# Window attention and MoE: one moving block for both parts of the probabilities, a full-width stationary block for global scores, interleaved first steps

## The chip, the cores and the metric

The kernel runs on one core of one Trainium2 chip. The metric is the device time in microseconds (us) of one execution; the time before is 1079.34 us, the median of three runs (1076.82 to 1079.34). Engines: PE is the matmul engine, DVE the vector engine, ACT the scalar engine, POOL the general one, and SP here only issues DMAs. Matmul results land in PSUM, which has 8 banks of 512 float32 columns on 128 partitions.

## The reference

Attention over 8 batches and 8 heads of 64 dimensions: 512 local tokens that see a window of 32 to each side and 32 global tokens, and 32 global tokens that see all 544. Its output goes through a feed-forward pair of layers (MoE in the names; there is one expert).

```python
k_all = np.concatenate([k_g, k_l], axis=2)
v_all = np.concatenate([v_g, v_l], axis=2)
s_g = scale * np.matmul(q_g, k_all.transpose(0, 1, 3, 2))
out_g = np.matmul(sm(s_g), v_all)
s_ll = scale * np.matmul(q_l, k_l.transpose(0, 1, 3, 2))
s_ll = np.where(np.abs(pos[:, None] - pos[None, :]) <= window, s_ll, -1e9)
s_lg = scale * np.matmul(q_l, k_g.transpose(0, 1, 3, 2))
out_l = np.matmul(sm(np.concatenate([s_lg, s_ll], axis=-1)), np.concatenate([v_g, v_l], axis=2))
x = np.concatenate([out_g, out_l], axis=2)   # then (batch * 544, 512)
h = x @ w_in                                 # 512 -> 2048
return ((h / (1.0 + np.exp(-h))) @ w_out)    # 2048 -> 512
```

## The kernel before

**Two strands on one PE queue.** The MoE runs over 34 tiles of 128 tokens, in a first block of one tile and eleven blocks of three (`SIZES`, L38). In a block, `first_layer` makes 128 of the 2048 hidden units at a time (16 rounds f) and `second_layer` of the round before adds them into the output banks. Attention makes the tiles of the next block meanwhile: 128 steps k, one for each batch b, chunk c of 128 queries and pair pr of heads.

**Split numbers.** Most operands are float32 that is split in a high part, rounded to the PE's fast float32 form, and the low rest; a product is then hi x hi + hi x lo + lo x hi. The first steps use plain float32 instead: scores until k = 28 (`ND`), values until k = 16 (`KF`), global scores until batch 3 (`GF`), and the first MoE block.

**A step.** `st_load` and `st_vload` fetch, `st_split` and `st_vsplit` split. `st_scores` makes the scores of two heads in bank s; DVE reduces and masks them (L351), ACT exponentiates, DVE and ACT normalize, and a DMA brings the probabilities into `rr`. `st_turn` transposes them into bank t; ACT writes the high part `pt_hi` (L403) and DVE the low part `pt_lo` (L404), POOL adds the 32 columns of global queries. `st_out` multiplies with the values: `vv` holds a chunk's values as 128 stationary columns, 64 high and 64 low. For each of two heads u and two key blocks a, a matmul of `vv` with `pt_hi` (L438) gives hi x hi on partitions 0 to 63 and lo x hi on 64 to 127, and a second one of the high values alone with `pt_lo` (L440) adds hi x lo. Both heads lie side by side in bank o. ACT copies the lower half out (L460), and DVE adds the upper one (L461) into `xs`, from which `xh` and `xl` are split (L462, L463).

**Heads of the global queries.** `g_load`, `g_split`, `g_scores` prepare a batch's global queries a batch ahead: three matmuls for each half of 272 keys (L245 to L247) in banks s and o, copied by ACT into `pgs` (L248). `g_soft` normalizes, `g_turn` transposes (gt in bank o, gu in bank s).

**Order.** PE's order is the program's. Each part of a step has a due time in steps (`DUE`, `HEAD`, `TURN`, `LATE`, L49 to L55), the stream is sorted by it, and `fill` issues what is due: by three parts after each first layer and by one after each output tile. So time in steps is spread over a block's matmuls. The other engines' orders are laid by a scheduler. In the first steps (k below 4) everything waits `LAG` more, and batch 0's global scores come after them. After the first block, banks s, t and o have one buffer each (`attbank`, L76); a step that needs a bank waits until DVE and ACT have emptied it.

**Weights.** 32 half loads of 512 KB, issued on ACT's queue (`fetch_weights`, L170), arrive as 64-bit words that `join_weights` makes into float32 on ACT (L196) and DVE (L198, L199).

Of the kernel before, what the change touches and what calls it, by code (L numbers as in the profile page):

```python
# [59 lines left out]
def attention_moe_kernel(ctx: ExitStack, tc: tile.TileContext, qk0_in, qk_in, v_in, gqk, wts, out):  # L60
# [63 lines left out]
    pts = []  # L124

    def pt_tiles(k):
        if not pts:
            for part in ("hi", "lo"):
                pts.append(work.tile([P, 2, 2, P + SG], F32R, tag=f"pt_{part}", name=f"pt_{part}"))
                nc.gpsimd.memset(pts[-1].bitcast(F32), 0.0)  # L130
        return pts

    def pt_whole(k):
        return work.tile([P, 2, 2, P + SG], F32, tag="pt_lo" if k % 2 else "pt_hi", name=f"pt{k}")
# [35 lines left out]
    def fetch_weights():  # L170
# [49 lines left out]
    def g_split(b, p):  # L220
        if b < GF:
# [3 lines left out]
        nc.scalar.copy(out=hi[:, :GW], in_=raw[:, :GW])  # L225
        nc.vector.tensor_tensor(out=lo, in0=raw[:, QG:GW], in1=hi[:, QG:GW].bitcast(F32), op=ALU.subtract)
        nc.vector.tensor_tensor(out=hi[:, GW : GW + QG], in0=raw[:, :QG], in1=hi[:, :QG].bitcast(F32),
                                op=ALU.subtract)
        state["gqk", p] = hi, lo

    def g_scores(b, p):
# [4 lines left out]
        else:  # L236
            hi, lo = state.pop(("gqk", p))
            qh, ql, kh = hi[:, :QG], hi[:, GW : GW + QG], hi[:, QG:GW]
        for j, kind in enumerate("so"):
            s = attbank(kind, f"gs{j}_{b}_{p}")  # L240
            ks = slice(j * GH, (j + 1) * GH)
            if b < GF:
                nc.tensor.matmul(s[:QG, :GH], raw[:, :QG], raw[:, QG:GW][:, ks], start=True, stop=True)  # L243
            else:
                nc.tensor.matmul(s[:QG, :GH], qh, kh[:, ks], start=True, stop=False)  # L245
                nc.tensor.matmul(s[:QG, :GH], qh, lo[:, ks], start=False, stop=False)
                nc.tensor.matmul(s[:QG, :GH], ql, kh[:, ks], start=False, stop=True)  # L247
# [479 lines left out]
```

## Time and profile before

| what | value |
|---|---|
| median of three runs | 1079.34 us |
| the profiled execution, its own time | 1074.63 us |
| its span in the profile | 1072.8 us |
| first MoE matmul | at 28.47 us |
| first matmul of the second block | at 110.39 us |
| mean granted PE clock | 0.989 |

A row of the timeline has the start in us, the busy time in us, engine, line, operation, out<-in, shape and count, and in brackets the idle time of the engine before it with what ended it. A matmul's shape is rows x stationary columns, then partitions x moving columns. A row of groups has the count, the total busy time in us and the mean in ns. Matmuls overlap in the pipeline, so the distance from one start to the next is what a matmul takes of PE's time. DVE's and ACT's rows overlap by less than 0.1 us.

### The profile page before, as it was taken

To read this page: it belongs to the slowest core of one execution; us is meant where nothing else is said; L and a number is where in the kernel's file an instruction comes from. 1 tells how busy PE (TensorE), PEld (TensorE's weight loads), DVE (VectorE), ACT (ScalarE), POOL (GpSimd) and SP (SyncE) were. 2 spreads that over 40 slices of the span, in tenths; PEclk is the share of its full clock that TensorE was granted. 3 is DMA by queue.
4 is the path that set the end of the run, shared out by engine and by line. 5 is a ranking of instruction groups with operands and counts; after the bars stand their busy time and mean duration, and the time that the engine had idled before them with its cause. 6 is when DMAs were issued, how large, how long until landed. Compare 5 with 4: busy or idle time off the path is not lost.

```text
span 1072.8 us, 19856 instructions
## 1 busy us (share of the span) xinstructions
PE 1037.6 (97%) x6168; PEld 929.6 (87%) x6168; DVE 748.4 (70%) x2285; ACT 735.1 (69%) x1977; POOL 189.0 (18%) x480
## 2 busy tenths in 40 slices
PE   6899989999999999999999999999999999999997
PEld 4676879889999899989999888999999999999996
DVE  3788756777788677786658877787877787664322
ACT  4788877777687677776558777777777777654322
POOL 2002766211111111111001111111111111110000
PEclk7999999999999999999999999999999999999999
DMA  7796232443343344333224334343433433310000
GB/s 258 242 320 207 90 94 79 130 138 100 109 147 118 100 135 129 111 114 104 76 76 150 127 98 130 113 124 123 128 111 115 152 105 113 115 40 21 30 1 29
DMA packets 67305, 126.01 MB, mean 117 GB/s; under 512 B 7552, under 2 KB 27520, under 8 KB 67200
## 3 DMA queue, kind: packets, MB, share of 16 engines
q1 hardware_dynamic: 62592, 107.97, 31.8%
q10 hardware_dynamic: 4608, 16.78, 4.5%
q8 instruction: 49, 0.80, 0.3%
q14 instruction: 56, 0.46, 0.1%
HBM read 86.44 MB, written 8.91 MB: 89 GB/s over the span
## 4 chain that ended last, share of the span: by engine, by line
PE 85%; ACT 5%; DVE 5%; DMA 2%; issue 2%; POOL 1%; SPq 0%; ACTq 0%; DVEq 0%
PE h L600 33%; PE out L625 11%; PE out L627 10%; PE out L626 10%; PE s L347 5%; PE o L438 4%; PE o L440 3%; PE t L382 3%; DMA raw<-in_qk_dram 1%; PE o L434 1%; PE h L594 1%; ACT probs L355 1%; PE gs L243 1%; ACT w_hi L209 1%; PE gt L281 1%
## 5 line engine op out<-in xcount | busy, mean ns | idle before, releaser
L600 PE MATMUL h<-xh,w_hi 128*128 128x384 f32 x704 | 241.5, 343 | 0.0
L600 PE MATMUL h<-xl,w_hi 128*128 128x384 f32 x704 | 238.5, 339 | 0.2 <-DVE xl L451 0.2
L600 PE MATMUL h<-xh,w_lo 128*128 128x384 f32 x704 | 238.3, 339 | 0.0
L625 PE MATMUL out<-w_hi,gh 128*128 128x512 f32 x528 | 219.0, 415 | 0.0
L627 PE MATMUL out<-w_hi,gl 128*128 128x512 f32 x528 | 208.5, 395 | 0.3 <-DVE gl L613 0.3
L626 PE MATMUL out<-w_lo,gh 128*128 128x512 f32 x528 | 207.8, 393 | 0.0
L606 ACT ACTIVATE t<-h 128x384 f32<-128x384 f32 (+1 forms) x192 | 90.8, 473 | 155.0 <-PE h L600 147.6
L608 DVE SCALAR_TENSOR_TENSOR t<-t,h 128x384 f32<-128x384 f32 x176 | 97.2, 552 | 108.0 <-ACT t L606 106.7
L600 PEld LDWEIGHTS h<-xl,w_hi 128*128 128x128 f32 x704 | 133.0, 189 | 5.9 <-DVE xl L451 0.5
L600 PEld LDWEIGHTS h<-xh,w_hi 128*128 128x128 f32 x704 | 132.9, 189 | 5.3
L600 PEld LDWEIGHTS h<-xh,w_lo 128*128 128x128 f32 x704 | 132.6, 188 | 0.0
L613 DVE TENSOR_TENSOR gl<-t,gh 128x384 fp32r<-128x384 f32 x176 | 100.4, 570 | 42.5 <-PE out L627 36.0
L355 ACT ACTIVATE probs<-probs,st 128x224 f32<-128x224 f32 x244 | 115.8, 476 | 9.3 <-DVE st L351 7.9
L406 POOL CAST pt_hi<-pgt 128x64 fp32r<-128x64 f32 x112 | 37.5, 335 | 478.2 <-PE o L440 334.5
L627 PEld LDWEIGHTS out<-w_hi,gl 128*128 128x128 f32 x528 | 99.2, 188 | 23.7 <-DVE gl L613 0.7
L351 DVE CUSTOM_DVE_ANT_0 probs<-s,mask 128x224 f32<-128x224 f32 x244 | 85.1, 384 | 44.2 <-PE s L347 39.2
L625 PEld LDWEIGHTS out<-w_hi,gh 128*128 128x128 f32 x528 | 99.7, 189 | 12.0 <-issue 1.6
L626 PEld LDWEIGHTS out<-w_lo,gh 128*128 128x128 f32 x528 | 100.0, 189 | 10.5
L612 ACT CAST gh<-t 128x384 fp32r<-128x384 f32 x176 | 89.8, 510 | 23.9 <-DVE t L608 21.2
L317 ACT CAST qk<-raw 128x704 fp32r<-128x704 f32 x100 | 78.0, 780 | 17.8 <-PE s L347 15.2
L461 DVE TENSOR_TENSOR xs<-o,xs 64x160 f32<-64x160 f32 x224 | 70.6, 315 | 26.9 <-ACT xs L460 22.6
L438 PE MATMUL o<-pt_hi,vv 128*128 128x160 f32 x448 | 87.8, 264 | 0.5 <-DVE xs L461 0.2
(120 smaller groups left out, 1878.3 us busy)
## 6 DMA issues: line engine op xcount, KB each, us to landing
raw<-in_qk_dram SPq DMA_DIRECT2D x100, 352.0 KB, 3.0
rr<-probs SPq DMA_DIRECT2D x112, 256.0 KB, 2.3
vraw<-in_v_dram SPq DMA_DIRECT2D x128, 128.0 KB, 2.3
raw_w<-in_wts_dram ACTq DMA_DIRECT2D x32, 512.0 KB, 6.3
raw_g<-in_gqk_dram SPq DMA_DIRECT2D x32, 304.0 KB, 2.9
out_dram<-o SPq DMA_DIRECT2D x32, 256.0 KB, 2.6
raw<-in_qk_dram SPq DMA_DIRECT2D x28, 240.0 KB, 4.0
out_dram<-o SPq DMA_DIRECT2D x8, 64.0 KB, 1.7
```

The costliest lines, as they stand in the source:

```text
L317: nc.scalar.copy(out=qk, in_=raw)
L351: nc.vector.tensor_tensor_reduce(out=p[:, u, :W], in0=s[:, u * W : (u + 1) * W], in1=mask_of[c], scale=-SCALE, scalar=3.0e38, op0=ALU.add, ...
L355: nc.scalar.activation(p[:, u, :W], p[:, u, :W], AF.Exp, bias=st[:, u : u + 1], scale=-1.0, accum_out=st[:, 2 + u : 3 + u])
L438: nc.tensor.matmul(o[:, at], vv[:, a, u].rearrange("p t d -> p (t d)"), pt_hi[:, u, a, :m], start=(a == 0), stop=(a == 1))
L600: nc.tensor.matmul(h[:, :nt], wt, x[:, c, :nt], start=(i == 0), stop=(i == 3 * NCC - 1))
L606: nc.scalar.activation(t[:, :nt], h[:, :nt], AF.Tanh, scale=0.5)
L608: nc.vector.scalar_tensor_tensor(out=out[:, :nt], in0=t[:, :nt], scalar=1.0, in1=h[:, :nt], op0=ALU.add, op1=ALU.mult)
L612: nc.scalar.copy(out=gh[:, :nt], in_=t[:, :nt])
L613: nc.vector.tensor_tensor(out=gl[:, :nt], in0=t[:, :nt], in1=gh[:, :nt].bitcast(F32), op=ALU.subtract)
L625: nc.tensor.matmul(o, gh[:, sl], wh, start=(f == 0), stop=False)
L626: nc.tensor.matmul(o, gh[:, sl], wl, start=False, stop=False)
L627: nc.tensor.matmul(o, gl[:, sl], wh, start=False, stop=(f == NF - 1))
```

## The change

Three parts, and due times.

Values: `pt_hi` and `pt_lo` become one tile `pt` that holds both parts side by side, and one matmul moves both through `vv`, 320 columns (256 where the second key block has no global part). Head u = 0 lands in bank o, u = 1 in bank s. hi x lo then stands in columns of its own, so that DVE has two adds for each head in place of one; lo x lo is made too and left unread.

Global scores: the queries' low and high parts make one stationary block of 128 columns, with two matmuls for each half. ACT copies the lower half, and DVE adds the upper.

First steps: a table gives each part of the first four steps, the first batch's global heads and four joins their own due times, and the first six weight loads go to SP's queue. gt moves from bank o to bank t.

```diff
-FIRSTC = {2: 1, 3: 1}
-LATE = dict(load=-1.0, first=0.2, head=0.8, soft=0.3, turn=1.0, slot=4.0)
-
-DUE = dict(load=-1.2, split=-0.5, vload=-0.6, vsplit=0.95, turn=1.6, out=2.2)
-LAG = 2.25
-HEAD = dict(load=-0.2, split=0.45, scores=0.65, soft=0.85, slot=0.3)
+
+FIRST = dict(load=(-1.2, -1.1, -1.0, 0.1), vload=(-0.9, 0.2, 0.3, 1.1), turn=(3.2, 4.0, 4.9, 5.8), out=(4.3, 5.2, 6.1, 7.0),
...
+DUE = dict(load=-1.2, split=-0.5, vload=-0.6, vsplit=0.95, turn=1.6, out=2.45)
+HEAD = dict(load=-0.2, split=0.6, scores=0.95, soft=1.15, slot=0.3)
-TURN = (0.7, 1.7)
+TURN = (1.3, 2.3)
...
-        load = nc.scalar.dma_start(out=w_raw[i], in_=wts[i // 2, :, sl].bitcast(I32))
+        load = queue.dma_start(out=w_raw[i], in_=wts[i // 2, :, sl].bitcast(I32))
...
-                nc.tensor.matmul(s[:QG, :GH], qh, kh[:, ks], start=True, stop=False)
-                nc.tensor.matmul(s[:QG, :GH], qh, lo[:, ks], start=False, stop=False)
-                nc.tensor.matmul(s[:QG, :GH], ql, kh[:, ks], start=False, stop=True)
-            nc.scalar.copy(out=pgs[p // 2][rows, ks], in_=s[:QG, :GH])
+                nc.tensor.matmul(s[:, :GH], both, kh[:, ks], start=True, stop=False)
+                nc.tensor.matmul(s[:, :GH], both, lo[:, ks], start=False, stop=True)
+                nc.scalar.copy(out=pg, in_=s[QG:, :GH])
+                nc.vector.tensor_tensor(out=pg, in0=s[:QG, :GH], in1=pg, op=ALU.add)
...
-        tb = attbank("o", f"gt{b}_{hh}")
+        tb = attbank("t", f"gt{b}_{hh}")
...
-                nc.tensor.matmul(o[:, at], vv[:, a, u].rearrange("p t d -> p (t d)"), pt_hi[:, u, a, :m],
-                                 start=(a == 0), stop=(a == 1))
-                nc.tensor.matmul(o[:D, at], vv[:, a, u, 0], pt_lo[:, u, a, :m], start=False, stop=(a == 1),
-                                 skip_group_check=(a == 1))
...
-        for u in range(2):
-            at = slice(u * wide, (u + 1) * wide)
+        for u, o in enumerate((o, attbank("s", f"os{k}"))):
+            o4 = o.rearrange("p (t q) -> p t q", t=2)
+            for a in range(2):
+                m = wide if a == 0 or c == NC - 1 else P
+                nc.tensor.matmul(o4[:, :, :m], vv[:, a, u].rearrange("p t d -> p (t d)"), pt[:, u, a, :, :m],
+                                 start=(a == 0), stop=(a == 1))
             rows = slice(D * u, D * (u + 1))
-            nc.scalar.copy(out=xs[rows, :], in_=o[D:, at])
-            nc.vector.tensor_tensor(out=xs[rows, :], in0=o[:D, at], in1=xs[rows, :], op=ALU.add)
+            nc.scalar.copy(out=xs[rows, :], in_=o4[D:, 0, :wide])
+            for t in range(2):
+                nc.vector.tensor_tensor(out=xs[rows, :], in0=o4[:D, t, :wide], in1=xs[rows, :], op=ALU.add)
```

What this does to the engines' orders is shown at three places. Lines are those of each kernel's own file (before: L347 scores, L438 and L440 out; after: L351 scores, L458 out); a row has the line, the operation, out<-in, and out's partitions x columns.

PE, around out of step 29, before: eight matmuls into bank o, and then the scores of step 31 in bank s.

```order
L438 MATMUL o29_2568<-pt_hi_1219,vv29_2444 128x160
L440 MATMUL o29_2568<-pt_lo_1221,vv29_2444 64x160
L438 MATMUL o29_2568<-pt_hi_1219,vv29_2444 128x160
...
L440 MATMUL o29_2568<-pt_lo_1221,vv29_2444 64x160
L347 MATMUL s31_2588<-qk31_2538 128x224
L347 MATMUL s31_2588<-klo31_2539,qk31_2538 128x224
```

The same place now: scores come first, and the four matmuls of out follow at once, two in bank o and two (os) in bank s.

```order
L351 MATMUL s31_2541<-qk31_2499 128x224
L351 MATMUL s31_2541<-klo31_2500,qk31_2499 128x224
L351 MATMUL s31_2541<-qk31_2499 128x224
L351 MATMUL s31_2541<-klo31_2500,qk31_2499 128x224
L458 MATMUL o29_2557<-pt_1203,vv29_2396 128x2x160 x2
L458 MATMUL os29_2559<-pt_1203,vv29_2396 128x2x160 x2
```

So two matmuls of out now have the scores' bank, which DVE's reductions of step 31 must have read.

DVE, the same step now: the reductions (L355), and behind them four adds into xs (L463) among other work, up to the next step's reductions.

```order
L355 ISA probs_115,st_2546<-s_2541,mask_105 128x224
L355 ISA st_2546 128x1
L610 SCALAR_TENSOR_TENSOR t_2_2534<-t_2_2534,h_2_2521 128x384
L322 TENSOR_TENSOR klo_2669<-raw_2620,qk_2668 128x448
L323 TENSOR_TENSOR qk_2668<-raw_2620,qk_2668 64x256
L463 TENSOR_TENSOR xs_2558<-o_2557,xs_2558 64x160
L361 TENSOR_SCALAR st_2546<-st_2546 128x2
L463 TENSOR_TENSOR xs_2558<-o_2557,xs_2558 64x160
L362 RECIPROCAL st_2546<-st_2546 128x2
L463 TENSOR_TENSOR xs_2558<-os_2559,xs_2558 64x160
```

The fourth add, from os again, stands three rows further on, behind a split of the values (L332). Before there were two such adds, both from bank o.

PE at the start, before: the rows from the last out of the first four steps to the second MoE matmul group (L594 is the MoE's first layer).

```order
L434 MATMUL o_277<-pt_267,vraw_222 64x128 x4
L594 MATMUL h_0_304<-x_214,w_180 128x128 x4
L243 MATMUL gs_0_2_313<-raw_g_2_269 64x272
L243 MATMUL gs_0_2_316<-raw_g_2_269 64x272
L594 MATMUL h_1_330<-x_214,w_293 128x128 x4
```

And now, from the last global scores on (L596 is the MoE's first layer):

```order
L246 MATMUL gs_0_3_286<-raw_g_3_215 64x272
L246 MATMUL gs_0_3_289<-raw_g_3_215 64x272
L435 MATMUL o_292<-pts,vraw_154 64x128 x4
L285 MATMUL gt_0_316<-ident,pg_123 128x128 x4
L288 MATMUL gu_0_322<-ident,pg_123 32x128
L435 MATMUL o_328<-pts,vraw_170 64x128 x4
L351 MATMUL s_337<-raw_299 128x224 x2
L596 MATMUL h_0_353<-x_239,w_223 128x128 x4
L596 MATMUL h_1_375<-x_239,w_282 128x128 x4
```

Global scores 2 and 3, the first gt and gu, and the scores of step 4 moved ahead of the first MoE matmul.

More of the change, by code (lines that the diff above doesn't have):

```diff
@@ L122, in attention_moe_kernel, with pt_tile @@
     pgs = [const.tile([P, SKV], F32, name=f"pg{i}") for i in range(2)]
-    pts = []
-    def pt_tiles(k):
+    pts, wholes = [], []
+    def pt_tile():
         if not pts:
[L128 to L131, printed above, removed]
+            pts.append(work.tile([P, 2, 2, 2, P + SG], F32R, tag="pt", name="pt"))
+            nc.gpsimd.memset(pts[0].bitcast(F32), 0.0)
+        return pts[0]
     def pt_whole(k):
-        return work.tile([P, 2, 2, P + SG], F32, tag="pt_lo" if k % 2 else "pt_hi", name=f"pt{k}")
+        if not wholes:
+            wholes.append(work.tile([P, 2, 2, 2, P + SG], F32, tag="pt", name="pts"))
+        return wholes[0][:, k % 2]
     def probs_tile(k):
@@ L224, in g_split @@
         hi, lo = qk_tiles(f"_g{b}_{p}")
[L225 to L228, printed above, removed]
+        nc.scalar.copy(out=hi[:, QG : QG + GW], in_=raw[:, :GW])
+        nc.vector.tensor_tensor(out=lo, in0=raw[:, QG:GW], in1=hi[:, 2 * QG : QG + GW].bitcast(F32), op=ALU.subtract)
+        nc.vector.tensor_tensor(out=hi[:, :QG], in0=raw[:, :QG], in1=hi[:, QG : 2 * QG].bitcast(F32), op=ALU.subtract)
         state["gqk", p] = hi, lo
@@ L424, in st_out @@
             vv = tiles.pop(("v", k))
-            pt_hi, pt_lo = pt_tiles(k)
+            pt = pt_tile()
         o = attbank("o", f"o{k}")
```

79 lines of the change are left out of this document (40 added, 39 removed).

## The prediction

> **What bounds the kernel now.** I read the page's busy shares first, then the windows by stage, then the waits of TensorE (PE), then the timeline around the places that the change touches.
>
> ```profile
> span 1072.8 us, 19856 instructions
> PE 1037.6 (97%) x6168; PEld 929.6 (87%) x6168; DVE 748.4 (70%) x2285; ACT 735.1 (69%) x1977; POOL 189.0 (18%) x480
> ```
>
> The windows (PE, weight load, DVE, ACT, POOL busy, granted clock, DMA share, GB/s) give three stages.
>
> ```profile
> 10.00:20.00 10.00, 5.00 (x23) 4.03 (x24) 4.38 (x15) 5.32 (x14) 0.00 (x0) 0.61 1.03 378
> 20.00:30.00 10.00, 9.27 (x45) 6.47 (x44) 1.73 (x5) 4.03 (x10) 0.00 (x0) 0.71 0.31 103
> 47.20:110.39 63.19, 59.22 (x342) 43.49 (x343) 53.39 (x203) 52.40 (x155) 11.23 (x27) 1.00 0.77 263
> 200.00:300.00 100.00, 99.70 (x614) 90.69 (x613) 78.36 (x242) 75.57 (x208) 16.68 (x48) 1.00 0.37 120
> ```
>
> The start has idle engines and a PE clock of 0.61 to 0.71; the first MoE block (to 110 us) is full on every engine; from there to about 1000 us PE is busy 99.7% and issues in an order fixed by the program, while DVE has some 22% left. So a matmul less there is time, and DVE work is free as long as no matmul comes to wait for it. The waits of PE after 110 us are few:
>
> ```profile
> PE gt L281 <- DVE xs L461: 5.8, 8, 2.0
> PE o L440 <- DVE pt_lo L404: 1.5, 2, 0.8
> ```
>
> **Fewer matmuls (term A, values).** A busy PE overlaps its own matmuls, so I take the distance from start to start.
>
> ```profile
> 255.26 0.27 PE L347 MATMUL s<-qk 128*128 128x224 f32 x1
> ...
> 255.59 0.27 PE L347 MATMUL s<-klo,qk 128*128 128x224 f32 x1
> ...
> 503.06 0.39 PE L626 MATMUL out<-w_lo,gh 128*128 128x512 f32 x1
> 503.29 0.40 PE L627 MATMUL out<-w_hi,gl 128*128 128x512 f32 x1
> ...
> 504.22 0.24 PE L438 MATMUL o<-pt_hi,vv 128*128 128x160 f32 x1
> ...
> 504.89 0.39 PE L600 MATMUL h<-xh,w_hi 128*128 128x384 f32 x1
> 505.11 0.34 PE L600 MATMUL h<-xl,w_hi 128*128 128x384 f32 x1
> 505.29 0.34 PE L600 MATMUL h<-xh,w_lo 128*128 128x384 f32 x1
> ```
>
> 512 columns take 0.23 us, 384 take 0.18, 224 take 0.11 (three steps in 0.33): about 0.015 us and 0.42 ns a column. A step's eight value matmuls take 504.89 - 504.22 = 0.67 us. They become two of 320 columns (0.148 us each on that line) and two of 256 (0.122): 0.54, so 0.13 less. In a batch's last four steps all eight have 160 columns:
>
> ```profile
> 220.09 0.24 PE L438 MATMUL o<-pt_hi,vv 128*128 128x160 f32 x1
> ...
> 220.80 0.30 PE L347 MATMUL s<-qk 128*128 128x224 f32 x1
> ```
>
> That is 0.71 against 4 x 0.148 = 0.59, so 0.12 less. 112 steps take this path (k from 16 to 127), 28 of them the wide one: 84 x 0.13 + 28 x 0.12 = **-14.3 us**.
>
> A rule speaks against this. The Trainium skill, "PSUM — Partial Sum Buffer", section "Specifications (TRN2)", says that any non-contiguous access pattern slows matmuls significantly, and the merged matmul writes two runs that lie 256 columns apart. No run here shows such a write; by that rule term A would become a loss, which is the last rival below.
>
> **Global scores (term B).** The 20 pairs of heads from batch 3 on, in two halves each, need two matmuls a half in place of three.
>
> ```profile
> L246 PE MATMUL gs<-klo_g,qk_g 128*64 128x272 f32 x40 | 11.4, 286 | 0.0
> 448.59 0.28 PE L246 MATMUL gs<-klo_g,qk_g 128*64 128x272 f32 x1
> 448.71 0.28 PE L247 MATMUL gs<-qk_g 128*64 128x272 f32 x1
> ```
>
> 40 matmuls go at 0.12 us from start to start: **-4.9 us**.
>
> **Waits that go (term C).** The transposes gt move to bank t, and turn to out grows from 0.6 to 0.85 of a step: 5.8 + 1.5 = **-7.3 us**. The bounds are -3 (gt finds bank t held instead) and -9.
>
> **DVE.** Each step gets two more adds of out's parts, and each of the 40 halves of global scores gets one:
>
> ```profile
> L461 DVE TENSOR_TENSOR xs<-o,xs 64x160 f32<-64x160 f32 x224 | 70.6, 315 | 26.9 <-ACT xs L460 22.6
> L248 ACT COPY pg<-gs 64x272 f32<-64x272 f32 x64 | 21.8, 380 | 2.4 <-PE gs L243 1.9
> ```
>
> 224 x 0.315 = 71 us, and 40 adds of 272 columns at about 0.4 us (an estimate between that row and the copy) = 16 us: 87 us over 890, which takes DVE from 78 to about 88%. I count them at nothing, covered by PE; what they cost where the cover fails is the next term and the second rival.
>
> **Waits that come (term E): bank s.** Scores, half of out, half of the global scores and gu now all take turns in bank s, which has one buffer. I counted in the order which matmuls stand between two users and summed their distances from the rows above, then set this cover against how long a bank takes to come free.
>
> ```profile
> 256.37 0.39 DVE L351 CUSTOM_DVE_ANT_0 probs<-s,mask 128x224 f32<-128x224 f32 x1
> 257.70 0.23 PE L440 MATMUL o<-pt_lo,vv 128*64 128x128 f32 x1
> 258.60 0.31 DVE L461 TENSOR_TENSOR xs<-o,xs 64x160 f32<-64x160 f32 x1
> 259.35 0.32 DVE L461 TENSOR_TENSOR xs<-o,xs 64x160 f32<-64x160 f32 x1
> 351.07 0.27 PE L284 MATMUL gu<-ident,pg 128*32 128x128 f32 x1
> 352.82 0.21 DVE L288 TENSOR_TENSOR pgl<-gu,pgh 32x64 fp32r<-32x64 f32 x1
> ```
>
> - Scores, then out's second half: the last scores matmul starts at 255.59, PE is past it at 255.70, and the second reduction ends at 256.76: 1.06 us. Of 97 places 13 have 0.3 us of matmuls between, 30 have 0.97, the others 1.66 or more: 13 x 0.76 + 30 x 0.09 = 12.6 us.
> - Out, then scores or global scores: 257.70 to 259.67 is 2.0 us, with two more adds 2.6. Of 109 places 9 have 1.7 or less, 3 have 2.4, the others 3.1 or more: 9 x 0.9 + 3 x 0.2 = 8.7 us.
> - gu, then out: 351.07 to 353.03 is 1.9 us. 5 places have about 0.3, 4 have 1.0: 5 x 1.6 + 4 x 0.9 = 11.6 us.
> - Global scores, then scores: a copy of 0.38, an add of 0.4, the hand-overs some 0.4: 1.2 us; 6 places have 0.94: 1.6 us.
>
> Singly that makes 34.5 us. They will not all show: what waits at one place is cover at the next. The same count can be tried on the gt that waits now. It stands behind out at 12 places, six with 1.7 us between and six with 2.4, and the second add ends 2.0 us (above) to 4.5 us after out:
>
> ```profile
> 355.09 0.24 PE L440 MATMUL o<-pt_lo,vv 128*64 128x160 f32 x1
> 359.37 0.32 DVE L461 TENSOR_TENSOR xs<-o,xs 64x160 f32<-64x160 f32 x1
> ```
>
> At 2.8, nearer the low end, it gives 6 x 1.1 + 6 x 0.4 = 9 us where the waits show 5.8, so I take six tenths: **+20 us**. The ends are 5 (the scheduler's order on DVE lets bank s go first) and 45 (each add delays what stands behind it on DVE: gl, STT, reductions).
>
> **Edits at nothing.** pt_hi and pt_lo become one tile, still with one buffer, and POOL clears it once with 1280 elements in place of twice 640; POOL's copies of the global part keep their place behind out. The later due times of the heads and of gt move scores, copies and adds within the same step and past no DMA; out is 0.25 of a step later, which is bank s's cover above. The last 70 us have no such step.
>
> **Start (term D).** In the order six weight loads leave ACT's queue for SP's, and two more joins, global scores 2 and 3, gt 0 and scores 4 stand ahead of the first MoE matmul.
>
> ```profile
> 17.40 0.68 ACT L196 ACTIVATE w<-raw_w 128x512 f32<-128x512 f32 x1 [0.48 <-DMA raw_w<-in_wts_dram]
> 28.47 1.23 PE L594 MATMUL h<-x,w 128*128 128x128 f32 x8
> 29.63 1.13 PE L243 MATMUL gs<-raw_g 128*64 128x272 f32 x4
> 32.53 2.04 PE L594 MATMUL h<-x,w 128*128 128x128 f32 x8 [1.77 <-DVE w L199]
> 40.51 0.63 PE L281 MATMUL gt<-ident,pg 128*128 128x128 f32 x4 [1.66 <-DVE pg L267]
> 41.94 0.92 PE L347 MATMUL s<-raw 128*128 128x224 f32 x4
> 47.22 1.16 PE L594 MATMUL h<-x,w 128*128 128x128 f32 x8 [0.81 <-DVE w L199]
> 110.39 0.42 PE L600 MATMUL h<-xh,w_hi 128*128 128x384 f32 x1
> ```
>
> From the first h to block 1 is 82 us. About 4 us of PE work leaves it (two global scores at 1.1 each, gt and its gu some 0.8, scores 0.9), and the three waits, 4.2 us, are for joins and a softmax that now come earlier. I let the first h come 2 us later, since PE is slow-clocked there: **-6 us**. At best (no later h, and ACT no longer held by a weight load at 17.40) -11; at worst +3: the weights now stand ahead of step 3's load on SP, 1.0 MB at the 378 GB/s of that window.
>
> **Sum.** On the profiled execution's 1074.63 us: -14.3 - 4.9 - 7.3 - 6 + 20 = -12.5, so 1062.1. The median of the runs shown, 1079.34, is 4.7 above that execution; I give the median: **1066.8 us**.
>
> **Rivals.**
> - The cover holds (E is 5, the start gives 9): 1074.6 - 26.5 - 9 + 5 + 4.7 = 1049. For it: DVE idles 22%, and the reductions after scores follow within 1.06 us. Against: 13 places with nothing between.
> - DVE and bank s set the pace, **slower**: DVE's order has waits of its own that cannot shrink (its longest, for the tanh, is below), so half of the 87 us shows, 43 us and more: 1074.6 - 32.5 + 48 + 4.7 = 1095 at 48. It decides from E = 33 on, where all gains are spent.
>
> ```profile
> DVE t L608 <- ACT t L606: 106.7, 102, 2.1
> ```
>
> - Break-even, E between 30 and 36: 1076 to 1082. The singly counted 34.5 us lies in it.
> - The merged matmul does not run at a column a step because its output is broken in two: at half pace 112 x 0.54 = +60 us, so 1066.8 + 60 = 1127. Against it: one break in 320 columns.
>
> **How the numbers follow.** Forecast 0.42 (1055 to 1075), cover 0.17, break-even 0.14, slower by DVE and bank s 0.23, broken write 0.04. Faster (by over 0.3%, about what a measurement of this kernel tells from no change) 0.59, same 0.14, slower 0.27. The range 1046 to 1092 leaves out the broken write and the far ends.
>
> **What would show it.** A and B: value matmuls some 0.54 us a step from first to next, no L247 of its own. C: no gt behind xs. E: new rows "os behind the reduction" and "s behind xs" in PE's waits, 20 us together; far above 33, or gl and the tanh's follower among them, and the slower rival holds. D: block 1's first matmul at about 104 us. DVE at 86 to 90% in the middle. A 320-column matmul that takes 0.25 us or more from start to start would break term A.

## The result and the profile after the change

The changed kernel takes 1115.16 us (median of 4 runs, 1113.51 to 1116.78), the kernel before it on the same chip 1078.09 us (4 runs): a ratio of 1.0344, 95% interval 1.0321 to 1.0367. It is **slower**, by 37 us, where 1066.8 us and a gain were forecast. The profiled execution took 1114.66 us, against 1074.63 us before.

The page's first lines for the changed kernel (span, then busy time, its share of the span and instructions of each engine):

```profile
span 1112.9 us, 18975 instructions
PE 1033.9 (93%) x5680; PEld 910.4 (82%) x5680; DVE 829.7 (75%) x2549; ACT 746.0 (67%) x1977; POOL 186.2 (17%) x479
```

PE issues 488 matmuls fewer (5680 against 6168), and its share falls from 97% to 93%: matmuls went, and idle time came. The windows of the steady part, with the columns of the prediction's windows, show where:

```profile
200.00:300.00 100.00, 95.13 (x528) 83.70 (x526) 80.69 (x254) 72.60 (x194) 14.38 (x46) 0.98 0.37 117
300.00:400.00 100.00, 92.44 (x525) 82.64 (x524) 83.83 (x260) 72.44 (x192) 13.72 (x45) 1.00 0.37 116
400.00:500.00 100.00, 96.37 (x548) 86.62 (x548) 87.51 (x271) 75.69 (x201) 15.37 (x47) 1.00 0.38 120
```

PE is idle for 4 to 8 us in each 100 where it was idle for 0.3 in the window shown before (up to 3.2 in the other windows from 200 to 900 us), and the first window's granted clock (the figure behind the five engines) is 0.98. The waits of PE name the place (us in total, times, longest):

```profile
PE os L458 <- DVE st L355: 23.6, 30, 2.5
PE os L458 <- DVE pgl L292: 19.8, 9, 3.0
...
PE s L351 <- DVE xs L463: 6.1, 11, 0.6
...
PE s L351 <- DVE pg L252: 2.4, 6, 0.5
PE gs L246 <- DVE xs L463: 1.5, 1, 1.5
```

The row "gt behind xs" (5.8 us before) is gone. In its place os, the second half of the output, waits 43.4 us in bank s: for the reductions that free the bank of the scores, and for the copy that frees it of gu. Two of these waits, row by row (start, duration, engine, line, output and input, and in brackets the idle time and what ended it). First the reductions:

```profile
437.39 0.62 DVE L322 TENSOR_TENSOR klo<-raw,qk 128x448 fp32r<-128x448 f32 x1
437.40 0.27 PE L351 MATMUL s<-klo,qk 128*128 128x224 f32 x1
...
438.03 0.43 DVE L323 TENSOR_TENSOR qk<-raw,qk 64x256 fp32r<-64x256 f32 x1
438.22 0.43 PE L458 MATMUL o<-pt,vv 128*128 128x320 f32 x2
438.49 0.72 DVE L266 TENSOR_REDUCE gst<-pg 128x1 f32<-128x544 f32 x1
...
439.43 0.39 DVE L355 CUSTOM_DVE_ANT_0 probs<-s,mask 128x224 f32<-128x224 f32 x1
...
439.88 0.54 PE L458 MATMUL os<-pt,vv 128*128 128x320 f32 x2 [1.23 <-DVE st L355]
```

The last scores matmul starts at 437.40, and the second reduction ends at 439.82, 2.4 us later. In the place of the kernel before that the prediction read, it was 1.17 us (255.59 to 256.76). The difference is what stands ahead of the reductions in DVE's order: two splits of the next queries and keys and a reduction of the global scores, 1.8 us of work that PE waited for nowhere before. Then gu:

```profile
501.24 0.27 PE L288 MATMUL gu<-ident,pg 128*32 128x128 f32 x1
...
502.05 0.43 PE L458 MATMUL o<-pt,vv 128*128 128x320 f32 x2
...
503.20 0.20 ACT L291 CAST pgh<-gu 32x64 fp32r<-32x64 f32 x1
503.42 0.48 ACT L363 ACTIVATE probs<-probs,st 128x224 f32<-128x224 f32 x1
...
504.24 0.60 ACT L634 ACTIVATE o<-out 128x512 f32<-128x512 f32 x1
...
504.86 0.20 ACT L291 CAST pgh<-gu 32x64 fp32r<-32x64 f32 x1
505.09 0.22 DVE L292 TENSOR_TENSOR pgl<-gu,pgh 32x64 fp32r<-32x64 f32 x1 [0.18 <-ACT pgh L291]
505.46 0.82 PE L458 MATMUL os<-pt,vv 128*128 128x320 f32 x2 [2.98 <-DVE pgl L292]
506.07 0.52 PE L602 MATMUL h<-xh,w_hi 128*128 128x384 f32 x1
506.39 0.52 PE L602 MATMUL h<-xl,w_hi 128*128 128x384 f32 x1
```

From gu's matmul to the end of the second pgl is 4.1 us, some 1.2 of it covered (up to 502.48, where the first half of the output ends). ACT has a softmax piece, the first half's own copy and a copy of a finished output between the two pieces of pgh. And after the wait PE runs slowly: the 384-column matmuls come at 0.32 us instead of 0.18. The windows there show the granted clock:

```profile
505.00:507.00 2.00, 1.54 (x5) 1.57 (x6) 0.54 (x2) 0.72 (x3) 0.56 (x2) 0.50 0.40 152
507.00:509.00 2.00, 2.00 (x8) 2.00 (x8) 1.03 (x3) 0.33 (x2) 0.21 (x1) 0.50 0.19 54
509.00:511.00 2.00, 2.00 (x10) 1.81 (x9) 0.27 (x1) 0.79 (x2) 0.00 (x0) 0.50 0.04 12
511.00:513.00 2.00, 2.00 (x9) 1.59 (x8) 0.92 (x2) 0.72 (x2) 0.00 (x0) 0.91 0.35 131
```

**The account.** The first matmul of block 1 comes at 102.1 us (110.4 before), 8.3 us earlier. From there to the end the changed kernel needs 1010.8 us against 962.4: 48.4 us more, though 19 us of matmuls were to go. The waits for a bank in the list above (23.6, 19.8, 6.1, 2.4, 1.5) are 53 us. The clock's deficit adds to them: over the eight windows from 100 to 900 us it reads 0.95, 0.98, 1.00, 1.00, 0.97, 1.00, 0.98 and 1.00, and 100 us at 0.95 lack 5 us of full speed, so 12 us in all, where the kernel before lacks 2. The waits of before, 5.8 and 1.5 us, are gone. 53 + 10 - 19 - 7 is 37 of the 48 us.

The rest lies in how a wait is counted. The bracket of a row begins at the modelled end of the matmul ahead, and that is later than the point where the next one could have started (a matmul of 512 columns lasts 0.40 us in its row, and the next starts after 0.23). So I also counted from start to start: each distance from one matmul to the next is set against the median of the same step. From block 1 to the last matmul that gives 924 us of matmuls at their own pace (941 before), 69 us of waits (13 before) and 12 us of slow clock (2 before): -17 + 55 + 10 = 48.

### The profile page after: what moved, and what is told of

The parts are those of the page before. It is cut to its first block, busy times and chain, and to the rows that moved or that the text cites. A ratio compares the mean times of both kernels' runs of the same rounds, so it can differ in the third digit from the quotient of the medians.

```text
span 1112.9 us, 18975 instructions
## 1 busy us (share of the span) xinstructions
PE 1033.9 (93%) x5680; PEld 910.4 (82%) x5680; DVE 829.7 (75%) x2549; ACT 746.0 (67%) x1977; POOL 186.2 (17%) x479
## 4 chain that ended last, share of the span: by engine, by line
PE 69%; DVE 12%; ACT 9%; issue 5%; DMA 3%; SPq 0%; ACTq 0%; DVEq 0%
PE h L602 28%; PE out L627 9%; PE out L629 9%; PE out L628 9%; PE s L351 4%; PE os L458 3%; PE t L386 2%; DVE xs L463 2%; DVE probs L355 2%; ACT t L608 2%; ACT probs L359 1%; PE o L458 1%; DMA raw_w<-in_wts_dram 1%; DVE gl L615 1%; ACT qk L321 1%
## 5 line engine op out<-in xcount | busy, mean ns | idle before, releaser
L628 PE MATMUL out<-w_lo,gh 128*128 128x512 f32 x528 | 210.2, 398 | 0.0
L615 DVE TENSOR_TENSOR gl<-t,gh 128x384 fp32r<-128x384 f32 x176 | 102.7, 584 | 42.4 <-PE out L629 38.9
L410 POOL CAST pt<-pgt 128x64 fp32r<-128x64 f32 x112 | 40.0, 357 | 542.2 <-PE os L458 519.5
L355 DVE CUSTOM_DVE_ANT_0 probs<-s,mask 128x224 f32<-128x224 f32 x244 | 85.4, 386 | 51.6 <-PE s L351 46.8
L458 PE MATMUL os<-pt,vv 128*128 128x320 f32 x224 | 54.9, 327 | 43.5 <-DVE st L355 23.6
L321 ACT CAST qk<-raw 128x704 fp32r<-128x704 f32 x100 | 78.0, 781 | 16.9 <-PE s L351 14.4
L463 DVE TENSOR_TENSOR xs<-os,xs 64x160 f32<-64x160 f32 x224 | 71.3, 318 | 15.7 <-ACT xs L461 8.9
```

The source lines that it names most:

```text
L355: nc.vector.tensor_tensor_reduce(out=p[:, u, :W], in0=s[:, u * W : (u + 1) * W], in1=mask_of[c], scale=-SCALE, scalar=3.0e38, op0=ALU.add, ...
L458: nc.tensor.matmul(o4[:, :, :m], vv[:, a, u].rearrange("p t d -> p (t d)"), pt[:, u, a, :, :m], start=(a == 0), stop=(a == 1))
L463: nc.vector.tensor_tensor(out=xs[rows, :], in0=o4[:D, t, :wide], in1=xs[rows, :], op=ALU.add)
L615: nc.vector.tensor_tensor(out=gl[:, :nt], in0=t[:, :nt], in1=gh[:, :nt].bitcast(F32), op=ALU.subtract)
L628: nc.tensor.matmul(o, gh[:, sl], wl, start=False, stop=False)
```

## The experiments

Three theories were held against one another. Theory 1: the shared bank s is the cost. Theory 2, its rival: the additions on VectorE are, whatever the bank. Theory 3, formed on the way: an addition costs where the bank that it reads is wanted within its hold, that is, the time until the last read of the bank has ended. The kernel before was timed again beside each group of experiments, on three chips; its medians were 1075.71 (e1 to e4), 1077.37 (e5 to e8), 1075.05 (e9 to e12) and 1074.08 us (e13), so that a difference of 3 us between groups means little.

### e1: the values undone

The eight matmuls of a step with one addition per head, all in bank o, as before, and `pt` is two tiles again. Global scores, start, due times and gt in bank t stay as changed. The core of the edit:

```diff
-        for u, o in enumerate((o, attbank("s", f"os{k}"))):
...
+                nc.tensor.matmul(o[:, at], vv[:, a, u]..., pt_hi[:, u, a, :m], start=(a == 0), stop=(a == 1))
+                nc.tensor.matmul(o[:D, at], vv[:, a, u, 0], pt_lo[:, u, a, :m], start=False, stop=(a == 1), ...)
...
-            for t in range(2):
-                nc.vector.tensor_tensor(out=xs[rows, :], in0=o4[:D, t, :wide], in1=xs[rows, :], op=ALU.add)
+            nc.vector.tensor_tensor(out=xs[rows, :], in0=o[:D, at], in1=xs[rows, :], op=ALU.add)
```

> The changed kernel with the value products put back to eight matmuls in one bank and one add per head; global scores, first steps, due times and gt in bank t stay changed. Bank theory (the halves of out in bank s wait for scores and gu): the 44 us of waits of os go, and the start (8 us) and global scores (5 us) stay as gains, so about 1060 us. DVE theory (the added adds delay all that stands behind them): the adds of out go too, so also about 1060. If it stays at 1090 or above, the loss is in the due times, in bank t or in the global scores, and both theories fall.

**1062.0 us**, ratio 0.9864 (0.9842 to 0.9885): faster than both. Of its windows one is enough (PE 99.64, clock 1.00):

```profile
300.00:400.00 100.00, 99.64 (x624) 91.41 (x623) 83.42 (x257) 78.45 (x216) 17.19 (x50) 1.00 0.41 130
```

PE hardly waits. So the values' part alone costs 1115 - 1062 = 53 us, and the rest of the change is a gain of some 14 us: the loss is not in the due times, in bank t or in the global scores. Between bank and additions this run does not decide, as was expected, since it takes both away. DVE is 83% busy in this window, as in the changed kernel's (83.83), but that window holds fewer steps; over the whole run DVE works 765 us here and 830 us in the changed kernel.

### e2: gu moved out of bank s

```diff
-TURN = (1.3, 2.3)
+TURN = (0.95, 1.95)
-        tb = attbank("s", f"gu{b}_{hh}")
+        tb = attbank("o", f"gu{b}_{hh}")
```

> The changed kernel with gu in bank o and the turns of the global queries due at 0.95 and 1.95 of a step (they were at 1.3 and 2.3). Bank theory: the 20 us in which os waits for gu's low part go, less a few us at bank o: about 1097 to 1102 us, with the 24 us of os behind the reductions unchanged. DVE theory: the waits only change their name, 1110 us or more.

1110.42 us, ratio 1.0318 (1.0276 to 1.0360). The bank theory's 1097 to 1102 is missed, and the time is the one that the DVE theory gave. The wait did not go. It moved to gt in bank t, since the earlier due time puts gt nearer behind the turn:

```profile
PE os L458 <- DVE st L355: 23.8, 30, 2.6
PE gt L285 <- DVE pt L409: 19.4, 13, 3.4
```

With three banks and one buffer in each, moving one user frees a place in one and takes it in another.

### e3: the kernel before with more additions

```diff
             nc.vector.tensor_tensor(out=xs[rows, :], in0=o[:D, at], in1=xs[rows, :], op=ALU.add)
+            nc.vector.tensor_tensor(out=xs[rows, :], in0=o[:D, at], in1=xs[rows, :], op=ALU.max)
```

> The kernel before with one more DVE instruction of 64x160 behind each add of out (a maximum with the same PSUM columns in place of nothing, so that out of the later steps is the larger of two numbers): 224 more of 0.315 us, DVE's load as in the changed kernel, no bank shared. DVE theory: slower by 25 us or more, 1103 or above. Bank theory: 1078 to 1086, a few us through bank o's later release.

1105.04 us, ratio 1.0253 (1.0218 to 1.0288): 29 us for 224 operations that the prediction had counted at nothing. Again the DVE theory's number came, and the bank theory's 1078 to 1086 did not. But the operations show as a wait of the next user of bank o (gt behind xs was 5.8 us before):

```profile
PE gt L281 <- DVE xs L462: 18.1, 12, 2.4
PE o L438 <- DVE xs L462: 4.4, 6, 1.1
```

### e4: the changed kernel with one addition

The product of the high part of the values with the low part of the probabilities is computed, but not added to the output.

```diff
-            for t in range(2):
-                nc.vector.tensor_tensor(out=xs[rows, :], in0=o4[:D, t, :wide], in1=xs[rows, :], op=ALU.add)
+            nc.vector.tensor_tensor(out=xs[rows, :], in0=o4[:D, 0, :wide], in1=xs[rows, :], op=ALU.add)
```

> The changed kernel with only the first of the two adds per head, so the high values times low probabilities are left out: DVE's load as before, bank s shared. Bank theory: os behind the reductions (24 us) and behind gu (20 us) stay, only s behind the adds (6 us) shrinks: 1100 to 1110 us. DVE theory: most of the loss goes, below 1085.

1103.38 us, ratio 1.0237 (1.0194 to 1.0281): 12 us less than the changed kernel. Both large waits stay as they were; those of the scores and global scores for xs are gone.

```profile
PE os L458 <- DVE st L355: 23.2, 30, 2.5
PE os L458 <- DVE pgl L292: 20.2, 9, 3.0
```

The bank theory's number came here. With as many additions as e1 and 14 us fewer matmuls by term A, it is 41 us slower than e1. So theory 2 does not hold for bank s: the larger part is the bank, not the additions.

### e5 and e6: the second half in bank t

e5 has both additions, e6 one (it leaves the same product out of the output as e4; the expectation below names it the other way round).

```diff
-DUE = dict(load=-1.2, split=-0.5, vload=-0.6, vsplit=0.95, turn=1.6, out=2.45)
-HEAD = dict(load=-0.2, split=0.6, scores=0.95, soft=1.15, slot=0.3)
+DUE = dict(load=-1.2, split=-0.5, vload=-0.6, vsplit=0.95, turn=1.6, out=2.15)
+HEAD = dict(load=-0.2, split=0.45, scores=0.65, soft=0.85, slot=0.3)
-TURN = (1.3, 2.3)
+TURN = (0.62, 1.62)
-        tb = attbank("t", f"gt{b}_{hh}")
+        tb = attbank("o", f"gt{b}_{hh}")
-        for u, o in enumerate((o, attbank("s", f"os{k}"))):
+        for u, o in enumerate((o, attbank("t", f"os{k}"))):
```

> The changed kernel, with the second half of the output (os) in bank t instead of bank s, the global transposes gt back in bank o as before, and the due times set for it (out 2.15, global turns 0.62 and 1.62, scores of the global heads 0.65). The matmuls of 320 columns and all three operations per head on VectorE and ScalarE stay. Theory 1 (what costs the time is that bank s, which scores, gu and gs take turns in, is now held by os too): the waits of os for the reductions (23.6 us) and for pgl (19.8) are gone, and the time is that of the version with the values undone (1062.0) minus the 14.3 us of term A plus 12 to 29 us for the additions: 1060 to 1077. Theory 2 (the additions on VectorE alone set the pace, whatever the bank): the time stays above 1090, with the waits now on t or o behind VectorE.

> The run before this one with the second addition of each head left out (so the product of the low part of the values and the high part of the probabilities... that is, one of the three partial products, is not added to the output; its matmul columns stay). It prices the additions with the shared bank gone: theory 1 says 8 to 15 us faster than the run with both additions (12 us is what the same cut gave with bank s shared), theory 2 says 25 us or more (29 us is what one such operation cost when put into the kernel before).

e5: 1128.36 us, ratio 1.0477 (1.0433 to 1.0521), slower than the change. e6: 1066.66 us, ratio 0.9899 (0.9850 to 0.9949). Theory 1 missed e5 by 50 us and e6's gain, 62 us where it said 8 to 15; theory 2 had both numbers. But e4 and e6 have the same matmuls and additions, and with the half in bank t in place of s (and the due times set for it) e6 is 37 us faster: that much is the bank's. The group of the turn's matmuls in the two (busy, mean ns, then the idle time ahead of them and what ended most of it), e5 first:

```profile
L386 PE MATMUL t<-ident,rr 128*128 128x128 f32 x448 | 54.9, 246 | 61.0 <-ACT gh L614 34.2 <-ACT probs L363 11.2 <-issue 7.3
```

```profile
L386 PE MATMUL t<-ident,rr 128*128 128x128 f32 x448 | 53.8, 243 | 14.4 <-DVE xs L462 14.0
```

The releasers named in e5 had long been done: in the row below gh had ended at 501.39, and the last addition of os, up to 501.97, is what still reads bank t.

```profile
501.65 0.32 DVE L463 TENSOR_TENSOR xs<-os,xs 64x160 f32<-64x160 f32 x1
...
502.07 0.51 PE L386 MATMUL t<-ident,rr 128*128 128x128 f32 x4 [1.81 <-ACT gh L614]
```

The same 224 additions thus cost 62 us here and 12 us in e4's place. The reading that fits both is the hold. From the traces I took, for each step, the time from the modelled end of the last output matmul to the end of the last addition: the median of 112 steps is 2.81 us in e5 and 1.46 in e6. In the order of these two kernels a quarter of the turns stand within 2.1 us of matmuls behind os. This is theory 3.

### e7 and e11: the output later

Only the due time of the output is changed: 2.7 in e7, 2.58 in e11.

```diff
-DUE = dict(load=-1.2, split=-0.5, vload=-0.6, vsplit=0.95, turn=1.6, out=2.45)
+DUE = dict(load=-1.2, split=-0.5, vload=-0.6, vsplit=0.95, turn=1.6, out=2.7)
```

> The changed kernel with the due time of the output 2.7 instead of 2.45, nothing else: os comes later after the scores of its bank, and nearer to the next scores. Theory 1 (the bank has no place for a fourth user, so a wait only moves): os behind the reductions falls from 23.6 to under 10 us, scores behind xs grows from 6.1 to 15 or more, and the time stays within 1100 to 1120. Rival (only the due time was badly chosen): under 1090.

e7: 1270.41 us, ratio 1.1793 (1.1716 to 1.1870), but not the experiment that was meant. The turn of the next step falls due at 2.6, ahead of the output at 2.7, so that the one tile pt is overwritten before the output reads it: the output of a step is computed with the next step's probabilities, and waits for them (`o behind pt`, 92.6 us). It says nothing on bank s.

> The changed kernel with the output's due time 2.58 instead of 2.45, so that the order of turn and output of the steps stays as it is (at 2.7 the next step's turn came ahead of the output, which then read the next step's probabilities). By the order, the cover of os behind scores in bank s has a median of 2.38 us instead of 1.66, that of scores behind os 3.81 instead of 4.51. Theory 1: a part of the waits of os for the reductions goes (23.6 to 10 to 15 us), and scores behind xs grow from 6.1 to 10 to 20: 1100 to 1118. Rival (the due time was badly chosen): under 1090.

e11: 1113.72 us, ratio 1.0352 (1.0330 to 1.0374), the same as the change within its interval.

```profile
PE s L351 <- DVE xs L463: 16.9, 16, 1.3
PE os L458 <- DVE pgl L292: 13.0, 6, 4.1
PE os L458 <- DVE st L355: 7.4, 12, 2.1
```

os waits 20.4 us instead of 43.4, the scores behind it 16.9 instead of 6.1: 12 us less. Other waits take 7 us of it (the list has 2.7 and 2.2 us of scores and global scores behind pt, new, and 4.6 instead of 2.4 behind pg), and the mean granted clock, 0.982 instead of 0.987, takes some 5. The clock's part lies ahead of block 1, which starts at 108.4 us here and at 102.1 in the changed kernel's trace (clock up to there 0.94 and 1.00). From block 1 on e11 needs 1002.5 us against 1010.8, so the later output may be worth some 8 us that the medians do not show. Most of the wait is moved from one turn of the bank to another, as theory 1 expected; the due time is a small part of the loss at most.

### e8: the global scores undone too

e1 with three matmuls on 64 stationary columns and one copy per half, without the addition. (The one tile that the expectation names is two tiles here, as in e1.)

```diff
-                nc.tensor.matmul(s[:, :GH], both, kh[:, ks], start=True, stop=False)
-                nc.tensor.matmul(s[:, :GH], both, lo[:, ks], start=False, stop=True)
-                nc.scalar.copy(out=pg, in_=s[QG:, :GH])
-                nc.vector.tensor_tensor(out=pg, in0=s[:QG, :GH], in1=pg, op=ALU.add)
+                nc.tensor.matmul(s[:QG, :GH], qh, kh[:, ks], start=True, stop=False)
+                nc.tensor.matmul(s[:QG, :GH], qh, lo[:, ks], start=False, stop=False)
+                nc.tensor.matmul(s[:QG, :GH], ql, kh[:, ks], start=False, stop=True)
+                nc.scalar.copy(out=pg, in_=s[:QG, :GH])
```

> The version with the values undone (1062.0), with the global scores undone as well (three matmuls on 64 stationary columns, one copy out of the bank, no addition). What is left of the change is the start, the due times, gt in bank t and the one tile for both parts. Term B as predicted (4.9 us of matmul time): 1067. Rival (the addition and the copy that B puts on VectorE give it back): 1060 to 1064.

1062.56 us, ratio 0.9869 (0.9826 to 0.9912), level with e1. Counted from start to start as above, e1's matmuls need 938 us against 941 in e8, and its waits 12 us against 8: what the matmuls gain goes back as waits. The longest of these is a row that e8's list lacks.

```profile
PE s L350 <- DVE pg L251: 2.5, 6, 0.5
```

The ratios' intervals are about 2 us (e1) and 5 us (e8) to either side, so a gain of 2 us would not be seen. What can be said is that term B is not worth the 4.9 us for certain, and may be worth nothing.

### e9 and e12: additions where the bank is free

e9 is e1 with the additional operation of e3. e12 is e1 again, beside it.

> The version with the values undone (1062.0), with one more 64x160 operation on VectorE (a maximum in place of the sum) behind each addition: about as many and as long operations as the changed kernel's second additions, but out of bank o, where between one output and the next user of the bank at least 4.7 us of other matmuls stand by the order. Theory 3 (an addition costs only where the bank that it reads is wanted within its hold, some 2.5 to 4 us): waits of o for xs stay under 6 us and the time is 1062 to 1070. Rival (80 us more on VectorE set the pace by themselves, as the 29 us in the kernel before might mean): 1080 or more.

> The version with the values undone once more, beside the three others on one chip: 1060 to 1064 (1062.0 before), so that the run with one wide half can be told from it at 3 us.

e9: 1079.43 us, ratio 1.0033 (1.0021 to 1.0045). e12: 1062.59 us, ratio 0.9879 (0.9860 to 0.9898). The 224 operations cost 17 us in e1, against 29 in the kernel before. That is 9 us over what theory 3 allowed and at the edge of what the rival expected. The rows:

```profile
PE gs L248 <- DVE xs L466: 5.6, 6, 2.2
PE o L441 <- DVE xs L466: 4.8, 7, 2.2
PE gs L245 <- DVE xs L466: 1.5, 2, 1.2
```

These are 11.9 us, where e1 waits 3.5 us for xs. From start to start all waits grow from 12 to 25 us, so most of the 17 us still lies on banks. The expectation spoke of 4.7 us of cover, and that holds from output to output only: the second half of the global scores uses bank o too, and where it waits in this trace it has 1.7 to 4.9 us, with one place of 6.1. The hold here is long, 4.0 us in the median where e1 has 2.6, and up to 7.9 us: it has two more additions in it, on a fuller DVE.

### e10 and e13: one wide half, in bank o

320 + 160 columns fit into one bank of 512. So only the first head of a step goes as a moving block of 320, the second in the form of before, and bank s has no fourth user.

```diff
+                if u == 0:
+                    nc.tensor.matmul(o4[:, :, :m], both, pt[:, u, a, :, :m], start=(a == 0), stop=(a == 1))
+                    continue
+                um = slice(2 * wide, 2 * wide + m)
+                nc.tensor.matmul(o[:, um], both, pt[:, u, a, 0, :m], start=(a == 0), stop=(a == 1))
+                nc.tensor.matmul(o[:D, um], vv[:, a, u, 0], pt[:, u, a, 1, :m], start=False, stop=(a == 1), ...)
```

> The changed kernel with only the first head of each step as matmuls of 320 columns, and the second in the form of before, all 480 columns in bank o, so that bank s has no fourth user; start, global scores and due times as in the changed kernel. Half of term A, 7 us, against 112 more additions out of a bank with 4.7 us of cover. Theory 3: 1053 to 1060, under the version with the values undone. Rival (additions cost by themselves, some 14 us for half of the 29): 1065 to 1072.

e10: 1392.11 us, ratio 1.2946 (1.2923 to 1.2969). It misses both expectations, by its own slip: the copies and additions of the first head stood ahead of the second head's matmuls in the code. In this program a write to a bank waits for the reads of it that the code has ahead, although they are of other columns:

```profile
PE o L465 <- DVE xs L471: 161.4, 87, 4.5
PE o L465 <- DVE st L362: 54.6, 21, 3.2
```

It is the changed kernel's cause in its purest form, a bank wanted while it is held, at each of 112 steps with no cover at all. e13 has all six matmuls first, and then the copies and additions:

> The one wide half once more, with all six matmuls of a step ahead of its copies and additions, as the kernel before has them; in the run before, the second head's matmuls were written behind the first head's additions, and, having the same bank, waited for them (161 us on xs alone). Half of term A, 7 us, off 1062.6, against 112 additions which, at the 17 us that some 220 of them cost out of this bank, are 8 us: 1060 to 1066, no gain over the values undone. Rival (the 17 us came late and are not halved, but gone, with half the operations): 1053 to 1058, which would beat it.

**1055.39 us**, ratio 0.9821 (0.9796 to 0.9847): the fastest of all, 7 us under e1 and e12 (about 6 by the ratios to the runs of before). The expected 1060 to 1066 is missed, and the rival's 1053 to 1058 met. Its rows from one step, and a window:

```profile
406.25 0.43 PE L460 MATMUL o<-pt,vv 128*128 128x320 f32 x2
406.51 0.24 PE L463 MATMUL o<-pt,vv 128*128 128x160 f32 x1
...
406.82 0.45 PE L636 MATMUL out<-w_hi,gh 128*128 128x512 f32 x1
```

```profile
300.00:400.00 100.00, 99.56 (x601) 91.21 (x600) 86.55 (x278) 79.53 (x219) 17.28 (x52) 1.00 0.41 132
```

The wide half takes 0.26 us, the other 0.31: 112 x 0.05 = 5.6 us of matmuls, and all of it shows. PE is at 99.56% in this window and DVE at 86.55%; over the whole run DVE works 784 us, against 765 in e1. The 112 more additions cost nothing that can be seen, so the price of an addition is not in proportion to their number.

**The runs counted one way.** From block 1 to the last matmul, from start to start as in the account above, in us, with DVE's work over the whole run beside it:

| run | matmuls at their pace | waits | slow clock | DVE's work |
|---|---|---|---|---|
| before | 941 | 13 | 2 | 748 |
| the change | 924 | 69 | 12 | 830 |
| e1, values undone | 938 | 12 | 0 | 765 |
| e3, before, more additions | 943 | 39 | 5 | 810 |
| e4, the change, one addition | 923 | 59 | 12 | 772 |
| e5, os in bank t | 921 | 83 | 9 | 829 |
| e6, os in bank t, one addition | 923 | 28 | 2 | 766 |
| e9, e1, more additions | 941 | 25 | 2 | 821 |
| e13, one wide half | 929 | 13 | 2 | 784 |

With 810 to 830 us of DVE's work PE waits between 25 and 83 us, and with 765 to 772 between 12 and 59. So the amount of DVE's work does not set the loss by itself; what does is which bank is held, and how soon it is wanted. This goes against theory 2 as it was put, although its numbers came in four experiments (e2, e3, e5, e6). Theory 3 is a reading that fits all runs, not a rule that forecast them: it was 9 us too low for e9 and 5 us too high for e13.

## Why the prediction was wrong

- **Term A, the matmuls (-14.3 us): right.** 320 columns go at 0.15 us from start to start in the changed kernel's trace, and 256 at 0.12, as read off the line of before; from e1 to the change the matmuls lose 14 us by the table. e13 got about half of it into the time. The rival of the broken write is refuted by the same figure: writing two runs of columns that lie 256 apart costs nothing that can be seen. On this the trace and the rule quoted from the Trainium skill, "PSUM — Partial Sum Buffer", section "Specifications (TRN2)", differ: by that rule the merged matmuls would have been a loss, so here the measurement decides.
- **Term B, global scores (-4.9 us): not confirmed.** e8 shows no difference in the time: some 3 us of matmuls go, and some 4 us of waits come. 2.5 us of these are scores that wait for the new addition; term E had them at 1.6.
- **Term C, waits that go (-7.3 us): right** for the part named: gt waits for xs no longer, in the changed kernel and in e1.
- **Term D, the start (-6 us): right in direction, its size open.** Block 1 starts 8.3 us earlier; in the experiments with the new start between 1.3 (e2) and 7.3 (e1). The mean clock ahead of block 1 was 0.92 in the trace of before, 1.00 in the changed kernel's and 0.93 to 0.97 in these experiments, and 0.08 of 110 us is as much as the gain. So part of the 8.3 us can be luck.
- **DVE's additions, counted at nothing: wrong as a rule.** 224 operations of 0.32 us cost 62 us (e6 to e5), 29 (e3), 17 (e9) or 12 (e4 to the change), and 112 of them nothing visible (e13). Their sum of 71 us is no guide. By theory 3 an addition costs what it lengthens the hold of a bank beyond its cover.
- **Term E, bank s (+20 us): the step that failed**, by its size. The sum of the other terms, -32.5 us, and the measured +40.0 of the two profiled executions leave 72 us for it, and 68 if term B is worth nothing. The trace shows 53 of these as waits for a bank (63 from start to start), all in the four kinds of place foreseen, and 10 us of clock over the kernel before. Three things were mis-sized:
  - Scores to out: 12.6 us forecast, 23.6 measured, at 30 places. The hold was read from one place, 255.59 to 256.76, where DVE happened to be free. With the splits ahead of the reductions it is 2.4 us (437.40 to 439.82), and 30 places wait 0.8 us each.
  - gu to out: 11.6 forecast, 19.8 measured, over the nine places that were counted. The 1.9 us from gu to pgl were again those of one place; with ACT's queue in between it is 4.1 (501.24 to 505.31).
  - The discount to six tenths. It came from one wait of the kernel before. Here the waits exceed the single count, 53 against 34.5, so nothing was to be taken off; that a DVE and an ACT that are late at one place are late at the next is likely, but not shown apart from the longer holds. Out to scores went the other way, 8.7 forecast and 7.6 measured (6.1 + 1.5).
- **The clock was not in the sum.** After the wait of 2.98 us PE ran at half clock up to 511.38, some 3 us lost, so that this wait cost about twice its length.
- The rival "DVE and bank s set the pace" was the right one in sign and place, with 1095 us from E = 48. It was given 0.23, and its sign, waits far above 33 us, came. Its mechanism was only half right: e9 gives DVE nearly as much work as the changed kernel (821 us against 830) and is 36 us faster.

Not settled: how much of the 53 us is due to DVE's order in the places with pgl, and whether another order of DVE and ACT around gu would save them; it was not tried. A version with both halves wide and a bank of its own was not tried either: the three attention banks are all taken.

## What to carry to other kernels

A matmul that is merged by writing to a second accumulator bank is paid in that bank's turns: before the columns are counted, list who else uses the bank, how long each holds it in the worst place (with what stands ahead of its release on the in-order engines, not in the best place of the trace), and how much other work stands between. An engine's idle share does not say whether work added to it is free; the next user of the buffer that this work releases does. And a half measure can beat the whole: one merged half that fits into the bank already held gained 19 us over the kernel before, together with the other parts, where both halves lost 37.

## What was not expected of the hardware

PE's granted clock fell to half after waits of some 2 us, and not after every one. Behind the wait of 2.98 us (505.46) 384 columns take 0.32 us from start to start instead of 0.18. In the clock record of this trace the stretches at 0.50 last 3.41 or 6.83 us (the last one is cut short by the end), and their starts, 112.02, 193.94, 255.38, 504.55, 777.62 and 907.32 us, lie whole multiples of 3.41 us apart, as on a grid. Two waits, each with a window of 2 us behind it:

```profile
254.21 0.50 PE L458 MATMUL os<-pt,vv 128*128 128x320 f32 x2 [2.10 <-DVE pgl L292]
```

```profile
256.00:258.00 2.00, 2.00 (x6) 1.54 (x6) 1.17 (x3) 0.65 (x2) 0.21 (x1) 0.50 0.47 160
```

```profile
372.21 0.54 PE L458 MATMUL os<-pt,vv 128*128 128x320 f32 x2 [1.94 <-DVE pgl L292]
```

```profile
374.00:376.00 2.00, 2.00 (x13) 1.79 (x12) 1.91 (x5) 0.97 (x3) 0.25 (x1) 1.00 0.42 149
```

The wait of 2.10 us lies in one window of the grid, 251.97 to 255.38, in which PE is busy for 1.31 us, and the next window is at half clock. The wait of 1.94 us is cut by the grid at 371.43, so that PE is busy for 2.25 us of the window ahead and for 2.64 us of the one behind, and the clock stays. That the length of a wait does not decide alone is seen in the kernel before, which has 2.01 us of idle time ahead of a gt at two places: at 359.83 it lies in one window (1.40 us busy) and half clock follows, at 623.75 it is cut by the grid (2.06 and 2.75 us busy) and none follows. From 40 us on, in the traces of before, of the change, of e3 and of e5, half clock followed each window at full clock with 1.81 us of idle time or more, and none with 1.74 or less; in the other traces it went either way between 1.57 and 1.83.

The Trainium skill, "TensorE: Matmul & The Clock Gate", section "Part 1: The HAM clock gate (the "warmup" mystery)", has the clock fall back after an idle window of about 3.4 us that runs freely. The window's length agrees with the 3.41 us here; that it has to be idle throughout does not, since 2.10 us of it were enough, and here the measurement decides. e1, whose longest wait after 110 us is 1.6 us, reads 1.00 in its windows of 100 us from 100 and from 300 us on.

The other thing is that a matmul whose output lies in two runs of 160 columns, 256 apart, went at the pace of one run: 0.15 us for 320 columns, as the line of before has it.
